# A fused adaLN attention block: the head's layernorm statistics, its order and its filler matmuls rearranged

## The chip, the cores and the metric

The kernel runs on one core of one Trainium2 chip. Its time is device microseconds of one execution, and the number that is compared is the median of several executions. A core has five engines that run their own instruction streams side by side: TensorE (PE; its weight loads are listed apart as PEld), VectorE (DVE), ScalarE (ACT), GpSimd (POOL) and SyncE (SP), which here only issues transfers. They meet at semaphores. 16 DMA engines move data between the main memory and the core's own memory (SBUF). TensorE writes into eight accumulation banks (PSUM), here `psbank0` to `psbank7`.

## What is computed

`x` is two batches of 256 tokens with 1152 channels, `c` one vector of 1152 for each batch; everything is bf16. The parts that matter:

```python
mod = (_silu(c) @ w_mod).reshape(B, 6, 1, D)
shift_a, scale_a, gate_a, shift_m, scale_m, gate_m = [mod[:, i] for i in range(6)]
h = _layernorm(x, axis=-1) * (1 + scale_a) + shift_a
qkv = h @ wqkv
...
p = _softmax(jnp.einsum('bqd,bkd->bqk', q, k) * D ** (-0.5), axis=-1)
a = jnp.einsum('bqk,bkd->bqd', p, v) @ wo
return x + gate_a * a
```

Only the first three of the six modulation vectors are used.

## The kernel before, in words

The 512 tokens are four tiles `i` of 128 rows (tiles 0 and 1 are batch 0, tiles 2 and 3 batch 1), and the 1152 channels are nine chunks `cc` of 128. Nothing is looped at run time: the program is written out instruction by instruction, in one Python function, and each engine runs its instructions in the order in which the function names them. A small helper (`_Prog`) records for every instruction what it reads and writes, and puts a wait wherever a value comes from another engine. For a PSUM bank it is stricter: whoever touches a bank waits for the last earlier access of every other engine to that bank. So the order around the change is the order of the calls in the source, and nothing else.

All loads are issued by SyncE in one list: four tiles of x, then, in four groups, the weights of the scale vector and the key weights of the same chunks ("ka"), then the shift weights, the remaining key weights, the query weights, the value weights. `c` is issued by ScalarE.

The head of the program, on which the change works, does this:

- `warm(n)` issues n matmuls of 512 columns on a tile of zeros into bank 4. Their result is not used. Before: five, then the nine tiny transposes of `c` (line 432), then nine more (all line 294).
- silu of `c`: a copy out of PSUM (`cT`), exp on ScalarE (`e1`), 1 + that on GpSimd (`d1`), a reciprocal on VectorE (`rc`) and a product on GpSimd (`scT`, line 457).
- Layernorm of tile i. `bn(i, q)` is VectorE's bn_stats over the third q of the channels (line 306). For tiles 1 to 3 the last third is taken by ScalarE instead: `third_act` gives the sum and the sum of squares (lines 312 and 314), and three tiny GpSimd steps, `third_end`, turn them into mean and sum of squared deviations (lines 318 to 322). Tile 0 takes all three thirds on VectorE. `aggr` merges the thirds (bn_aggr, line 330), `rstd` is a logarithm and an exp on ScalarE (lines 334 and 337), and `xn(i)` normalizes the tile on VectorE (line 341).
- `xT(i)` transposes the nine chunks of tile i on TensorE (line 349). Chunks 0 to 7 go to bank 5 for even tiles and bank 6 for odd ones, chunk 8 of every tile to bank 7. `xT_out(i, half, engine)` copies four chunks out of the bank (lines 300 on VectorE, 302 on ScalarE), and `xT_last(b, engine)` copies chunk 8 of both tiles of a batch. Tile 2 uses bank 5 again, so its transposes wait for both evacuations of tile 0; its ninth transpose goes to bank 7 and waits for `xT_last(0)`.
- `s_mm(g)` are the modulation matmuls for the scale vector, group g, two columns each (line 367), into bank 7; `s_ev` reads them and adds 1 (line 378); `scale_x` multiplies a transposed chunk of one batch with it (line 399 on VectorE, 401 on GpSimd, 403 on ScalarE).
- The key matmuls (line 419) follow: first chunks k = 0 and 1 of batch 0 (ten of 256 columns), then after the transposes of tiles 2 and 3 and `s_mm(1)` the same for batch 1 (ten of 256), then eleven of 512 columns, and so on through all chunks, with `s_mm` and the shift vector's `h_mm` between them.

The shift is added later (for queries and values); the queries, values, scores, softmax, the product with v, the output projection with the gate and the stores follow in one long run of matmuls.

Of the kernel before, what the change touches and what calls it, by code (L numbers as in the profile page):

```python
# [21 lines left out]
class _Prog:  # L22
# [12 lines left out]
    def op(self, eng, fn, r=(), w=(), dma=False, extra=()):  # L35
        o = _Op()
        o.eng, o.fn, o.dma = eng, fn, dma
        o.sem = o.val = None
        o.inc = False
        deps = set(extra)  # L40
        for k in r:
            if k[0] == "ps":
                continue
            p = self.last_w.get(k)
            if p is not None and not (p.eng == eng == PE):
                deps.add(p)
# [127 lines left out]
def _build(nc, es, x, c, wqkv, wo, w_mod, out):  # L174
# [33 lines left out]
    s1_sb = sb("s1_sb", [P, DC, 2], f32)  # L208
    sh_sb = sb("sh_sb", [P, DC, 2], f32)
    gaterow_sb = sb("gaterow_sb", [P, GW], bf16)  # L210
    stat_sb = sb("stat_sb", [P, TT, 6, 3], f32)
    sums_sb = sb("sums_sb", [P, TT, 2], f32)
    sq_sb = sb("sq_sb", [P, TT], f32)
    mv_sb = sb("mv_sb", [P, TT, 2], f32)
# [71 lines left out]
        out=ident[:, :], in_=ident[:, :], compare_op=ALU.not_equal, fill=1.0,  # L286
        base=0, pattern=[[-1, P]], channel_multiplier=1), r=[("ident",)], w=[("ident",)])
    op(POOL, lambda g: g.memset(eps_sb[:, :], EPS_B), w=[("eps",)])
    op(POOL, lambda g: g.memset(stat_sb[:, 1:TT, 4, 0:1], 384.0), w=[("cnt",)])
    op(POOL, lambda g: g.memset(scT_sb[:, :, :], 0.0), w=[("scT",)])  # L290

    def warm(n, bank=4):
        for _ in range(n):
            op(PE, lambda pe: pe.matmul(ps[bank][:, 0:512], warm_sb[:, 0:P], warm_sb[:, 0:512],  # L294
                                        start=True, stop=True),
               r=[("warm",)], w=[("ps", bank)])

    def evac(eng, dst, src, r, w):
        if eng == DVE:
            op(DVE, lambda v: v.tensor_copy(dst, src), r=r, w=w)  # L300
        else:
            op(AC, lambda a: a.activation(dst, src, ACT.Copy), r=r, w=w)  # L302


    def bn(i, q):
        op(DVE, lambda v: v.bn_stats(  # L306
            stat_sb[:, i, 2 * q:2 * q + 2, :].rearrange("p a b -> p (a b)"),
            x_sb[:, i, q * 384:(q + 1) * 384]), r=[("x", i)], w=[("stat", i, q)])

    def third_act(i):  # L310
        src = x_sb[:, i, 768:1152]
        op(AC, lambda a: a.activation(junk_sb[:, 0, :], src, ACT.Copy, accum_out=sums_sb[:, i, 0:1]),
           r=[("x", i)], w=[("junk", 0), ("sum", i)])
        op(AC, lambda a: a.activation(junk_sb[:, 1, :], src, ACT.Square, accum_out=sums_sb[:, i, 1:2]),  # L314
           r=[("x", i)], w=[("junk", 1), ("sq", i)])

    def third_end(i):
        op(POOL, lambda g: g.tensor_scalar(stat_sb[:, i, 4, 1:2], sums_sb[:, i, 0:1], 1.0 / 384, 0.0,
                                           op0=ALU.mult, op1=ALU.add), r=[("sum", i)], w=[("tm", i)])
        op(POOL, lambda g: g.tensor_tensor(sq_sb[:, i:i + 1], sums_sb[:, i, 0:1], sums_sb[:, i, 0:1],  # L320
                                           ALU.mult), r=[("sum", i)], w=[("s2", i)])
        op(POOL, lambda g: g.tensor_scalar(stat_sb[:, i, 4, 2:3], sq_sb[:, i:i + 1], -1.0 / 384,  # L322
                                           sums_sb[:, i, 1:2], op0=ALU.mult, op1=ALU.add),
           r=[("s2", i), ("sq", i)], w=[("tv", i)])

    def aggr(i, third):
        n = 5 if third else 6
        need = [("stat", i, 0), ("stat", i, 1)]
        need += [("tm", i), ("tv", i), ("cnt",)] if third else [("stat", i, 2)]
        op(DVE, lambda v: v.bn_aggr(mv_sb[:, i, :], stat_sb[:, i, 0:n, :].rearrange("p a b -> p (a b)")),  # L330
           r=need, w=[("mv", i)])

    def rstd(i):
        op(AC, lambda a: a.activation(lnv_sb[:, i:i + 1], mv_sb[:, i, 1:2], ACT.Ln,  # L334
                                      bias=eps_sb[:, 0:1], scale=1.0),
           r=[("mv", i), ("eps",)], w=[("lnv", i)])
        op(AC, lambda a: a.activation(rstd_sb[:, i:i + 1], lnv_sb[:, i:i + 1], ACT.Exp, scale=-0.5),
           r=[("lnv", i)], w=[("rstd", i)])

    def xn(i):  # L340
        op(DVE, lambda v: v.tensor_scalar(xo_sb[:, i, :], x_sb[:, i, :], mv_sb[:, i, 0:1],
                                          rstd_sb[:, i:i + 1], op0=ALU.subtract, op1=ALU.mult),
           r=[("x", i), ("mv", i), ("rstd", i)], w=[("xo", i)])

    def xT(i):
        for cc in range(DC):
            bank = (5 + i % 2) if cc < 8 else 7
            lo = cc * P if cc < 8 else 512 + i * P
            op(PE, lambda pe, cc=cc, bank=bank, lo=lo: pe.transpose(  # L349
                psb[bank][:, lo:lo + P], xo_sb[:, i, cc * P:(cc + 1) * P], ident[:, :]),  # L350
               r=[("xo", i), ("ident",)], w=[("ps", bank)])
# [20 lines left out]
    def s_mm(g):  # L372
        mod_mm(s_ap(g), [("ws", g)], *SGROUPS[g], 0)
# [18 lines left out]
    def scale_x(cc, b, eng):  # L392
        dst = h0T_sb[:, cc, b * NTOK:(b + 1) * NTOK]
        src = xnT_sb[:, cc, b * NTOK:(b + 1) * NTOK]
        sc = s1_sb[:, cc, b:b + 1]
        rk = [("xnT", cc, 2 * b), ("xnT", cc, 2 * b + 1), ("s1", cc)]
        wk = [("pv", cc, b)]
        if eng == DVE:
            op(DVE, lambda v: v.tensor_scalar(dst, src, sc, None, op0=ALU.mult), r=rk, w=wk)  # L399
# [24 lines left out]


    op(AC, lambda a: a.preload_act_table_set("natural_log_exp_and_others"))
    warm(5)

    def f_cT(pe):
        last = None  # L430
# [3 lines left out]
        return last  # L434
    op(PE, f_cT, r=[("c",), ("ident",)], w=[("ps", 0)])
    cT_ps = psb[0][:, 0:2 * DC].rearrange("p (k b) -> p k b", b=2)
    op(DVE, lambda v: v.tensor_copy(cT_sb[:, :, :], cT_ps), r=[("ps", 0)], w=[("cT",)])
    op(AC, lambda a: a.activation(e1_sb[:, :, :], cT_sb[:, :, :], ACT.Exp, scale=-1.0),
       r=[("cT",)], w=[("e1",)])
    warm(9)  # L440

    bn(0, 0)
    bn(0, 1)
    bn(0, 2)
    third_act(1)
    aggr(0, False)
    op(POOL, lambda g: g.tensor_scalar(d1_sb[:, :, :], e1_sb[:, :, :], 1.0, 1.0, op0=ALU.mult, op1=ALU.add),
       r=[("e1",)], w=[("d1",)])
    bn(1, 0)
    bn(1, 1)  # L450
    third_end(1)
    rstd(0)
    aggr(1, True)
    xn(0)
    rstd(1)
    op(DVE, lambda v: v.reciprocal(rc_sb[:, :, :], d1_sb[:, :, :]), r=[("d1",)], w=[("rc",)])
    op(POOL, lambda g: g.tensor_tensor(scT_sb[:, :, 0:2], cT_sb[:, :, :], rc_sb[:, :, :], ALU.mult),
       r=[("cT",), ("rc",)], w=[("scT",)])
    xn(1)
    third_act(2)  # L460
    bn(2, 0)
    bn(2, 1)
    third_end(2)
    xT(0)
    xT(1)
    s_mm(0)
    xT_out(0, 0, AC)
    xT_out(1, 0, DVE)
    s_ev(0)
    scale_x(0, 0, DVE)  # L470
    scale_x(1, 0, DVE)
    aggr(2, True)
    rstd(2)
    third_act(3)
    bn(3, 0)
    xn(2)
    bn(3, 1)
    third_end(3)
    aggr(3, True)
    rstd(3)  # L480
    xT_out(0, 1, AC)
    xn(3)
    xT_out(1, 1, DVE)
    xT_last(0, AC)

    for k in range(2):
# [248 lines left out]
```

## Time and profile before

| what | value |
|---|---|
| three runs, device time | 105.62, 104.95, 105.29 us |
| median | 105.29 us |
| the profiled execution, its own time | 105.28 us |
| its span, first to last instruction | 103.4 us |
| TensorE busy | 94.3 us (91%), 728 matmuls |
| VectorE, ScalarE, GpSimd busy | 44.8, 25.2, 8.7 us |
| mean granted TensorE clock over the span | 0.967 |
| DMA traffic | 21.65 MB, mean 209 GB/s |

The profile is one execution. Its times are microseconds from the first instruction, and line numbers are those of the kernel before. "Granted clock" is the share of full speed that TensorE's clock was given; where the records hold nothing earlier, the first stretch stands as full. A row of a timeline gives start, length, engine, line, operation, the tile written and those read, sizes, and the number of instructions merged; in square brackets stands how long the engine was idle before, and what ended that. A few matmul records can be missing. The chain of work that ended last is followed backward from the last instruction, at each step to whatever released it.

### The profile page before, as it was taken

How to read it: one execution, taken by the hardware profiler on the slowest of the kernel's cores; microseconds unless marked ns; L12 is line 12 of the kernel's file. 1: busy time of each engine (PE TensorE's matmuls, PEld its weight loads, DVE VectorE, ACT ScalarE, POOL GpSimd, SP SyncE). 2: the span in 40 equal slices, each digit the busy share in tenths (PEclk: the TensorE clock that was granted, in tenths of full speed). 3: DMA queues.
4: the chain of work that ended last, by engine and by line, in shares of the span. 5: the costliest groups of instructions: out<-in, count | busy, mean ns of one | idle time of the engine just before them, and what ended most of it. 6: DMA issues, size and time to landing. Idle time of an engine off the chain costs nothing.

```text
span 103.4 us, 1795 instructions
## 1 busy us (share of the span) xinstructions
PE 94.3 (91%) x728; PEld 55.8 (54%) x734; DVE 44.8 (43%) x122; ACT 25.2 (24%) x64; POOL 8.7 (8%) x30
## 2 busy tenths in 40 slices
PE   5956458999999999999999999999999999999990
PEld 2324356354545445454445688665667866666570
DVE  1598746012406905050372115660342755676572
ACT  4374584001105020000232135433103730000000
POOL 4022202001403004040000000000000000000000
PEclk9999985579999999999999999999999999999999
DMA  2999999999999999999999400002777666764122
GB/s 48 296 331 337 335 326 334 363 324 322 344 356 341 357 332 390 391 393 391 390 394 390 182 1 10 0 0 8 21 21 34 34 41 41 23 137 139 47 75 76
DMA packets 20076, 21.65 MB, mean 209 GB/s; under 512 B 866, under 2 KB 16098, under 8 KB 20068
## 3 DMA queue, kind: packets, MB, share of 16 engines
q1 hardware_dynamic: 20064, 21.53, 75.4%
q8 instruction: 6, 0.10, 0.4%
q10 hardware_dynamic: 4, 0.00, 0.1%
q14 instruction: 2, 0.02, 0.1%
HBM read 19.76 MB, written 1.18 MB: 203 GB/s over the span
## 4 chain that ended last, share of the span: by engine, by line
PE 83%; DMA 6%; DVE 3%; ACT 2%; SPq 2%; issue 1%; POOL 0%; POOLq 0%
PE psbank L419 35%; PE psbank L579 17%; PE psbank L685 17%; DMA wm_sb<-in_w_mod_dram 6%; PE psbank L592 4%; PE psbank L660 4%; PE psbank L367 4%; SPq L252 2%; PE psbank L637 1%; PE psbank L349 1%; DVE pvT_sb L399 1%; DVE ga_sb L692 1%; ACT lnv_sb L334 1%; DVE xo_sb L695 0%; ACT junk_sb L314 0%
## 5 line engine op out<-in xcount | busy, mean ns | idle before, releaser
L419 PE MATMUL psbank<-pvT_sb,wq_sb 128*128 128x512 bf16 (+1 forms) x88 | 20.6, 393 | 1.4 <-DVE pvT_sb L399 1.0
L579 PE MATMUL psbank<-wq_sb,hT_sb 128*128 128x384 bf16 x108 | 18.2, 326 | 0.1
L685 PE MATMUL psbank<-wm_sb,pvT_sb 128*128 128x384 bf16 (+2 forms) x117 | 17.7, 314 | 0.0
L419 PE MATMUL psbank<-hT_sb,wq_sb 128*128 128x512 bf16 x78 | 17.5, 379 | 0.1
L419 PEld LDWEIGHTS psbank<-pvT_sb,wq_sb 128*128 128x128 bf16 x91 | 9.5, 108 | 10.7 <-issue 2.4
L685 PEld LDWEIGHTS psbank<-wm_sb,pvT_sb 128*128 128x128 bf16 x117 | 11.2, 98 | 6.5
L579 PEld LDWEIGHTS psbank<-wq_sb,hT_sb 128*128 128x128 bf16 x108 | 10.5, 98 | 7.0 <-issue 0.2
L419 PEld LDWEIGHTS psbank<-hT_sb,wq_sb 128*128 128x128 bf16 x81 | 7.8, 98 | 9.1
L302 ACT ACTIVATE qkT_sb<-psbank 128x512 bf16<-128x512 f32 x8 | 4.3, 597 | 25.0 <-PE psbank L419 21.6
L692 DVE TENSOR_TENSOR ga_sb<-psbank,gate_rep 128x384 bf16<-128x384 f32 (+2 forms) x13 | 6.8, 527 | 6.1 <-PE psbank L685 6.1
L300 DVE CAST qkT_sb<-psbank 128x512 bf16<-128x512 f32 x10 | 6.3, 685 | 5.7 <-PE psbank L419 5.6
L300 DVE CAST v_sb<-psbank 128x384 bf16<-128x384 f32 x6 | 3.2, 555 | 10.9 <-PE psbank L579 10.9
L367 PEld LDWEIGHTS psbank<-scT_sb,wm_sb 128*128 128x128 bf16 x162 | 5.1, 97 | 1.6 <-POOL stat_sb L322 0.5
L294 PE MATMUL psbank<-warm_sb 128*128 128x512 bf16 x14 | 4.9, 506 | 1.2 <-DVE warm_sb L283 1.2
L349 PE MATMUL psbank<-ident,xo_sb 128*128 128x128 bf16 x36 | 2.6, 225 | 3.4 <-ACT xnT_sb L302 2.2
L367 PE MATMUL psbank<-scT_sb,wm_sb 128*128 128x2 bf16 x162 | 5.1, 164 | 0.3 <-DMA wm_sb<-in_w_mod_dram 0.3
L387 DVE COPY sh_sb<-psbank 128x6 f32<-128x6 f32 x3 | 0.5, 165 | 11.3 <-PE psbank L367 11.3
L302 ACT ACTIVATE v_sb<-psbank 128x384 bf16<-128x384 f32 x6 | 2.9, 487 | 9.8 <-PE psbank L579 9.8
L695 DVE TENSOR_TENSOR xo_sb<-x_sb,ga_sb 128x384 bf16<-128x384 bf16 (+2 forms) x13 | 4.5, 343 | 0.5
L306 DVE BATCH_NORM_STATS2 stat_sb<-x_sb 128x6 f32<-128x384 bf16 x9 | 4.5, 535 | 0.0
L378 DVE TENSOR_SCALAR s_sb<-psbank 128x4 f32<-128x4 f32 (+1 forms) x4 | 0.6, 160 | 8.8 <-PE psbank L367 8.8
L413 POOL TENSOR_SCALAR hT_sb<-pvT_sb,sh_sb 128x256 bf16<-128x256 bf16 x6 | 3.2, 533 | 14.8 <-DVE sh_sb L387 14.8
(57 smaller groups left out, 68.8 us busy)
## 6 DMA issues: line engine op xcount, KB each, us to landing
wm_sb<-in_w_mod_dram SPq DMA_DIRECT2D x4, 864.0 KB, 9.4
wq_sb<-in_wqkv_dram SPq DMA_DIRECT2D x4, 672.0 KB, 10.6
wq_sb<-in_wqkv_dram SPq DMA_DIRECT2D x3, 864.0 KB, 10.8
wm_sb<-in_w_mod_dram SPq DMA_DIRECT2D x1, 2592.0 KB, 15.9
wm_sb<-in_wo_dram SPq DMA_DIRECT2D x1, 2592.0 KB, 15.4
wm_sb<-in_w_mod_dram SPq DMA_DIRECT2D x3, 576.0 KB, 7.6
wq_sb<-in_wqkv_dram SPq DMA_DIRECT2D x3, 448.0 KB, 8.3
x_sb<-in_x_dram SPq DMA_DIRECT2D x4, 288.0 KB, 3.9
```

Of the source, the lines that this page charges most:

```text
L294: op(PE, lambda pe: pe.matmul(ps[bank][:, 0:512], warm_sb[:, 0:P], warm_sb[:, 0:512], start=True, stop=True), r=[("warm",)], w=[("ps", bank)])
L300: op(DVE, lambda v: v.tensor_copy(dst, src), r=r, w=w)
L302: op(AC, lambda a: a.activation(dst, src, ACT.Copy), r=r, w=w)
L306: op(DVE, lambda v: v.bn_stats(stat_sb[:, i, 2 * q:2 * q + 2, :].rearrange("p a b -> p (a b)"), x_sb[:, i, q * 384:(q + 1) * 384]), r=[("x ...
L367: op(PE, lambda pe, cc=cc, k=k: pe.matmul(ps[7][:, col + 2 * cc:col + 2 * cc + 2], src[:, k, (cc - a) * P:(cc - a + 1) * P], scT_sb[:, k, ...
L419: op(PE, lambda pe: pe.matmul(ps[bank][:, lo:hi], wq_sb[:, k, col * P:(col + 1) * P], src[:, k, lo:hi], start=(k == 0) if start is None el ...
L579: op(PE, lambda pe, k=k, q=q, bank=bank: pe.matmul(ps[bank][:, 0:384], hT_sb[:, k, i * P:(i + 1) * P], wq_sb[:, k, 2 * D + q * 384:2 * D + ...
L592: op(PE, lambda pe, cc=cc: pe.matmul(ps[bank][:, 0:NTOK], qkT_sb[:, cc, i * P:(i + 1) * P], qkT_sb[:, DC + cc, b * NTOK:(b + 1) * NTOK], s ...
L660: op(PE, lambda pe, h=h, cc=cc, sbk=sbk: pe.matmul(ps[bank][:, h * NTOK:(h + 1) * NTOK], v_sb[:, 2 * b + sbk, cc * P:(cc + 1) * P], pT_sb[ ...
L685: op(PE, lambda pe, i=i, k=k, c0=c0, c1=c1, n=n, bank=bank: pe.matmul(ps[bank][:, 0:n], pvT_sb[:, k, i * P:(i + 1) * P], wo_ap[:, k, c0:c1 ...
L692: op(DVE, lambda v, b=b, c0=c0, c1=c1, n=n, bank=bank, s=s: v.tensor_tensor(ga_sb[:, s, 0:n], ps[bank][:, 0:n], gate_rep[:, b, c0:c1], ALU ...
L695: op(DVE, lambda v, i=i, c0=c0, c1=c1, n=n, s=s: v.tensor_tensor(xo_sb[:, i, c0:c1], x_sb[:, i, c0:c1], ga_sb[:, s, 0:n], ALU.add), r=[("x ...
```

## The change

It does five things, all in the head.

1. Tile 0 is handled like the others: its last third goes to ScalarE and GpSimd, so `aggr` has one form and `stat_sb` five entries instead of six. `third_act` is called for one sum at a time.
2. `cT` is copied out of PSUM by ScalarE instead of VectorE, and `d1` follows at once.
3. The calls between c's transposes and the transposes of tile 2 are in another order: the statistics of tiles 2 and 3 come ahead of the evacuations and scales of batch 0, `rc` and `scT` come behind `xn(1)`, and `rstd(2)` stands before `xT_out(1, 0)`.
4. `xT_out(1, 1)` goes to ScalarE instead of VectorE; for batch 1, `xT_out(3, 1)` is called before `xT_out(2, 1)`.
5. The fillers become 4 + 13 + 2 + 3 instead of 5 + 9. The two stand ahead of `s_mm(0)`, the three behind it, ahead of batch 0's keys.

```diff
-    warm(5)
+    warm(4)
...
-    op(DVE, lambda v: v.tensor_copy(cT_sb[:, :, :], cT_ps), r=[("ps", 0)], w=[("cT",)])
+    evac(AC, cT_sb[:, :, :], cT_ps, [("ps", 0)], [("cT",)])
...
-    warm(9)
+    op(POOL, lambda g: g.tensor_scalar(d1_sb[:, :, :], e1_sb[:, :, :], 1.0, 1.0, op0=ALU.mult, op1=ALU.add),
+       r=[("e1",)], w=[("d1",)])
+    warm(13)
 
     bn(0, 0)
     bn(0, 1)
-    bn(0, 2)
-    third_act(1)
-    aggr(0, False)
...
+    third_act(0, 0)
+    third_act(0, 1)
+    third_end(0)
     bn(1, 0)
     bn(1, 1)
+    third_act(1, 0)
+    third_act(1, 1)
     third_end(1)
+    aggr(0)
     rstd(0)
-    aggr(1, True)
+    bn(2, 0)
+    third_act(2, 0)
+    aggr(1)
     xn(0)
     rstd(1)
+    xn(1)
...
-    xn(1)
-    third_act(2)
-    bn(2, 0)
+    third_act(2, 1)
+    third_end(2)
+    third_act(3, 0)
+    third_act(3, 1)
+    third_end(3)
     bn(2, 1)
-    third_end(2)
+    bn(3, 0)
+    aggr(2)
+    bn(3, 1)
     xT(0)
     xT(1)
+    warm(2)
     s_mm(0)
+    warm(3)
     xT_out(0, 0, AC)
+    rstd(2)
     xT_out(1, 0, DVE)
     s_ev(0)
     scale_x(0, 0, DVE)
     scale_x(1, 0, DVE)
-    aggr(2, True)
-    rstd(2)
-    third_act(3)
-    bn(3, 0)
     xn(2)
-    bn(3, 1)
-    third_end(3)
-    aggr(3, True)
+    aggr(3)
     rstd(3)
     xT_out(0, 1, AC)
     xn(3)
-    xT_out(1, 1, DVE)
+    xT_out(1, 1, AC)
     xT_last(0, AC)
...
+    xT_out(3, 1, DVE)
     xT_out(2, 1, AC)
-    xT_out(3, 1, DVE)
```

What this does to the engines' streams, in three places. Each row is a line of the source, the operation, what it writes and reads, its size, and how many follow each other. The lines of the kernel after are four lower in the helpers (330 is 326, 341 is 337, 378 is 374, 399 is 395, 334 is 330, 349 is 345, 367 is 363, 419 is 415).

VectorE, from the normalization of tile 0 or 1 to that of tile 3, before (`xo_sb` is the normalized tile, `mv_sb` its mean and variance, `stat_sb` the statistics of the thirds, `s_sb` the scale vector plus 1, `pvT_sb` the scaled chunk that the keys read):

```order
L456 RECIPROCAL rc_sb<-d_sb 128x18
L341 TENSOR_SCALAR xo_sb<-x_sb,mv_sb,rstd_sb 128x1152
L306 BN_STATS stat_sb<-x_sb 128x6 x2
L300 COPY xnT_sb<-psbank 128x4x128
L378 TENSOR_SCALAR s_sb<-psbank 128x4
L399 TENSOR_SCALAR pvT_sb<-xnT_sb,s_sb 128x256 x2
L330 BN_AGGR mv_sb<-stat_sb 128x2
L306 BN_STATS stat_sb<-x_sb 128x6
L341 TENSOR_SCALAR xo_sb<-x_sb,mv_sb,rstd_sb 128x1152
L306 BN_STATS stat_sb<-x_sb 128x6
L330 BN_AGGR mv_sb<-stat_sb 128x2
L341 TENSOR_SCALAR xo_sb<-x_sb,mv_sb,rstd_sb 128x1152
```

and VectorE at the same place after:

```order
L337 TENSOR_SCALAR xo_sb<-x_sb,mv_sb,rstd_sb 128x1152 x2
L458 RECIPROCAL rc_sb<-d_sb 128x18
L306 BN_STATS stat_sb<-x_sb 128x6 x2
L326 BN_AGGR mv_sb<-stat_sb 128x2
L306 BN_STATS stat_sb<-x_sb 128x6
L300 COPY xnT_sb<-psbank 128x4x128
L374 TENSOR_SCALAR s_sb<-psbank 128x4
L395 TENSOR_SCALAR pvT_sb<-xnT_sb,s_sb 128x256 x2
L337 TENSOR_SCALAR xo_sb<-x_sb,mv_sb,rstd_sb 128x1152
L326 BN_AGGR mv_sb<-stat_sb 128x2
L337 TENSOR_SCALAR xo_sb<-x_sb,mv_sb,rstd_sb 128x1152
```

The statistics of tiles 2 and 3 moved ahead of batch 0's evacuation, scale vector and scales; between batch 0's scales and the last normalization only tile 2's normalization and tile 3's aggregate are left.

ScalarE, from the evacuation of tile 0's first half to the end of batch 0's evacuations, before (`lnv_sb` and `rstd_sb` are the logarithm and the exp of a tile, `sums_sb` ScalarE's sums):

```order
L302 ACTIVATE xnT_sb<-psbank 128x4x128
L334 ACTIVATE lnv_sb<-mv_sb,eps_sb 128x1
L337 ACTIVATE rstd_sb<-lnv_sb 128x1
L312 ACTIVATE junk_sb,sums_sb<-x_sb 128x384
L314 ACTIVATE junk_sb,sums_sb<-x_sb 128x384
L334 ACTIVATE lnv_sb<-mv_sb,eps_sb 128x1
L337 ACTIVATE rstd_sb<-lnv_sb 128x1
L302 ACTIVATE xnT_sb<-psbank 128x4x128
L302 ACTIVATE xnT_sb<-psbank 128x256
```

and ScalarE at the same place after:

```order
L313 ACTIVATE junk_sb,sums_sb<-x_sb 128x384 x3
L302 ACTIVATE xnT_sb<-psbank 128x4x128
L330 ACTIVATE lnv_sb<-mv_sb,eps_sb 128x1
L333 ACTIVATE rstd_sb<-lnv_sb 128x1
L330 ACTIVATE lnv_sb<-mv_sb,eps_sb 128x1
L333 ACTIVATE rstd_sb<-lnv_sb 128x1
L302 ACTIVATE xnT_sb<-psbank 128x4x128 x2
L302 ACTIVATE xnT_sb<-psbank 128x256
```

Tile 3's sums moved ahead of the first evacuation, and two halves instead of one (tile 0's and tile 1's) stand between tile 3's rstd and the last chunk.

TensorE, from behind c's transposes to the transposes of tiles 2 and 3, after (before, the rows of 2 and 3 fillers are absent and the first row has 9):

```order
L294 MATMUL psbank<-warm_sb 128x512 x13
L345 MATMUL psbank<-ident,xo_sb 128x128 x18
L294 MATMUL psbank<-warm_sb 128x512 x2
L363 MATMUL psbank<-scT_sb,wm_sb 128x2 x18
L294 MATMUL psbank<-warm_sb 128x512 x3
L415 MATMUL psbank<-pvT_sb,wq_sb 128x256 x10
L345 MATMUL psbank<-ident,xo_sb 128x128 x18
```

Fillers now stand on both sides of the modulation matmuls; the order of all other matmuls is unchanged.

More of the change, by code (lines that the diff above doesn't have):

```diff
@@ L210, in _build @@
     gaterow_sb = sb("gaterow_sb", [P, GW], bf16)
-    stat_sb = sb("stat_sb", [P, TT, 6, 3], f32)
+    stat_sb = sb("stat_sb", [P, TT, 5, 3], f32)
     sums_sb = sb("sums_sb", [P, TT, 2], f32)
@@ L288, in _build @@
     op(POOL, lambda g: g.memset(eps_sb[:, :], EPS_B), w=[("eps",)])
-    op(POOL, lambda g: g.memset(stat_sb[:, 1:TT, 4, 0:1], 384.0), w=[("cnt",)])
+    op(POOL, lambda g: g.memset(stat_sb[:, :, 4, 0:1], 384.0), w=[("cnt",)])
     op(POOL, lambda g: g.memset(scT_sb[:, :, :], 0.0), w=[("scT",)])
@@ L308, in bn, with third_act @@
             x_sb[:, i, q * 384:(q + 1) * 384]), r=[("x", i)], w=[("stat", i, q)])
-    def third_act(i):
+    def third_act(i, kind):
         src = x_sb[:, i, 768:1152]
[L312 to L315, printed above, removed]
+        fn = (ACT.Copy, ACT.Square)[kind]
+        op(AC, lambda a: a.activation(junk_sb[:, kind, :], src, fn, accum_out=sums_sb[:, i, kind:kind + 1]),
+           r=[("x", i)], w=[("junk", kind), ("sum" if kind == 0 else "sq", i)])
     def third_end(i):
@@ L324, in third_end, with aggr @@
            r=[("s2", i), ("sq", i)], w=[("tv", i)])
[L326 to L331, printed above, removed]
+    def aggr(i):
+        op(DVE, lambda v: v.bn_aggr(mv_sb[:, i, :], stat_sb[:, i, :, :].rearrange("p a b -> p (a b)")),
+           r=[("stat", i, 0), ("stat", i, 1), ("tm", i), ("tv", i), ("cnt",)], w=[("mv", i)])
     def rstd(i):
@@ L436, in _build @@
     cT_ps = psb[0][:, 0:2 * DC].rearrange("p (k b) -> p k b", b=2)
-    op(DVE, lambda v: v.tensor_copy(cT_sb[:, :, :], cT_ps), r=[("ps", 0)], w=[("cT",)])
+    evac(AC, cT_sb[:, :, :], cT_ps, [("ps", 0)], [("cT",)])
     op(AC, lambda a: a.activation(e1_sb[:, :, :], cT_sb[:, :, :], ACT.Exp, scale=-1.0),
        r=[("cT",)], w=[("e1",)])
-    warm(9)
+    op(POOL, lambda g: g.tensor_scalar(d1_sb[:, :, :], e1_sb[:, :, :], 1.0, 1.0, op0=ALU.mult, op1=ALU.add),
+       r=[("e1",)], w=[("d1",)])
+    warm(13)
     bn(0, 0)
     bn(0, 1)
-    bn(0, 2)
-    third_act(1)
-    aggr(0, False)
-    op(POOL, lambda g: g.tensor_scalar(d1_sb[:, :, :], e1_sb[:, :, :], 1.0, 1.0, op0=ALU.mult, op1=ALU.add),
-       r=[("e1",)], w=[("d1",)])
+    third_act(0, 0)
+    third_act(0, 1)
+    third_end(0)
     bn(1, 0)
     bn(1, 1)
+    third_act(1, 0)
+    third_act(1, 1)
     third_end(1)
+    aggr(0)
     rstd(0)
-    aggr(1, True)
+    bn(2, 0)
+    third_act(2, 0)
+    aggr(1)
     xn(0)
     rstd(1)
+    xn(1)
     op(DVE, lambda v: v.reciprocal(rc_sb[:, :, :], d1_sb[:, :, :]), r=[("d1",)], w=[("rc",)])
```

## The prediction

> **What bounds the kernel now.** I read the slices of the page first, then the chain of work that ended last in order of time, then a table of TensorE's busy time by stretch, then the timelines of single engines.
>
> From the page: the busy tenths of TensorE and its granted clock, 40 slices of 2.585 us each.
>
> ```profile
> PE   5956458999999999999999999999999999999990
> PEclk9999985579999999999999999999999999999999
> ```
>
> From slice 7 on TensorE is full. Before that it has gaps, and in slices 6 to 9 its clock is far below full. So the end is set by when the dense stream starts and how fast it runs at first. The chain in order of time (start, length, what) names the place:
>
> ```profile
> 3.16 5.87 DMA wm_sb<-in_w_mod_dram
> ...
> 12.91 0.30 ACT lnv_sb L334
> ...
> 13.98 1.20 PE psbank L349 x17
> ...
> 15.21 0.44 DVE xnT_sb L300
> ...
> 15.67 0.30 DVE pvT_sb L399
> ...
> 16.01 2.31 PE psbank L419 x10
> ...
> 18.54 3.90 PE psbank L419 x10
> 22.44 0.43 PE psbank L367 x18
> ...
> 25.91 0.65 PE psbank L367 x27
> ...
> 26.64 4.48 PE psbank L419 x20
> ```
>
> Batch 1's chain runs through tile 3's rstd, the evacuation that frees a bank, the transposes of tiles 2 and 3 (13.98), an evacuation, a scale, and batch 1's first key matmuls (16.01). From there PE is never idle for long. The rows of 512-column keys differ: 20 matmuls of 512 columns take 4.48 us (0.224 each), while the 11 issued between 18.32 and 22.44 (the program's count; one record is missing) take 4.12. The next table gives per stretch: its length, then busy time and (instructions) of PE, PEld, DVE, ACT, POOL, the clock, the DMA share and GB/s. The edges are where the clock changes, and steps of 3.41 us from there.
>
> ```profile
> 1.29:4.70 3.41, 3.41 (x17) 1.18 (x17) 0.83 (x3) 1.61 (x3) 0.75 (x5) 1.00 0.81 223
> 4.70:8.12 3.42, 2.28 (x17) 1.02 (x15) 3.27 (x10) 2.66 (x11) 0.90 (x5) 1.00 1.02 322
> 8.12:11.53 3.41, 2.27 (x37) 1.94 (x37) 2.78 (x10) 1.70 (x7) 0.53 (x3) 1.00 1.10 331
> 11.53:14.95 3.42, 1.22 (x20) 0.98 (x18) 1.85 (x5) 2.22 (x9) 0.61 (x3) 0.99 1.13 329
> 14.95:18.36 3.41, 3.09 (x32) 2.33 (x31) 2.02 (x7) 1.66 (x4) 0.56 (x1) 0.50 1.08 340
> 18.36:21.77 3.41, 3.23 (x8) 1.21 (x8) 0.00 (x0) 0.00 (x0) 0.00 (x0) 0.51 1.08 356
> ```
>
> The stretch 11.53 to 14.95 is the emptiest on TensorE, and the clock is half for the 6.82 us behind it. The same table for the key matmuls alone (line 419; PE, PEld, clock, DMA):
>
> ```profile
> 8.12:11.53 3.41, 1.01 (x10) 0.90 (x10) 1.00 1.10 331
> 11.53:14.95 3.42, 0.24 (x3) 0.00 (x0) 0.99 1.13 329
> 14.95:18.36 3.41, 2.31 (x10) 1.64 (x12) 0.50 1.08 340
> ```
>
> A stretch with 1.01 us of keys held the clock, one with 0.24 lost it. TensorE's own timeline gives the rates:
>
> ```profile
> 1.19 2.31 PE L294 MATMUL psbank<-warm_sb 128*128 128x512 bf16 x5 [1.19 <-DVE warm_sb L283]
> ...
> 7.38 1.47 PE L349 MATMUL psbank<-ident,xo_sb 128*128 128x128 bf16 x18 [1.08 <-DVE xo_sb L341]
> ...
> 10.52 1.25 PE L419 MATMUL psbank<-pvT_sb,wq_sb 128*128 128x256 bf16 x10 [0.77 <-DVE pvT_sb L399]
> ...
> 15.07 0.67 PE L367 MATMUL psbank<-scT_sb,wm_sb 128*128 128x2 bf16 x18
> ```
>
> Ten keys of 256 columns take 1.25 us here and 2.31 at half clock. The first fillers take 0.46 each, half rate too, though the clock column says 1.00 there. Eighteen modulation matmuls take 0.67 at half clock.
>
> **The change, step by step.** Rows for VectorE, ScalarE and GpSimd:
>
> ```profile
> 3.95 1.47 DVE L306 BATCH_NORM_STATS2 stat_sb<-x_sb 128x6 f32<-128x384 bf16 x3
> 5.45 0.24 DVE L330 BATCH_NORM_AGGREGATE mv_sb<-stat_sb 128x2 f32<-128x18 f32 x1
> ...
> 7.24 0.26 DVE L456 RECIPROCAL rc_sb<-d_sb 128x18 f32<-128x18 f32 x1
> 7.49 0.63 DVE L341 TENSOR_SCALAR xo_sb<-x_sb,mv_sb,rstd_sb 128x1152 bf16<-128x1152 bf16 x1
> 8.04 1.00 DVE L306 BATCH_NORM_STATS2 stat_sb<-x_sb 128x6 f32<-128x384 bf16 x2
> 8.97 0.40 DVE L300 COPY xnT_sb<-psbank 128x512 bf16<-128x512 bf16 x1
> 9.79 0.16 DVE L378 TENSOR_SCALAR s_sb<-psbank 128x4 f32<-128x4 f32 x1 [0.41 <-PE psbank L367]
> 9.98 0.48 DVE L399 TENSOR_SCALAR pvT_sb<-xnT_sb,s_sb 128x256 bf16<-128x256 bf16 x2
> ```
> ```profile
> 4.59 0.52 ACT L312 ACTIVATE junk_sb<-x_sb 128x384 bf16<-128x384 bf16 x1 [0.30 <-DMA x_sb<-in_x_dram]
> ...
> 13.34 0.85 ACT L302 ACTIVATE xnT_sb<-psbank 128x512 bf16<-128x512 bf16 x2
> ```
> ```profile
> 12.35 0.27 POOL L322 TENSOR_SCALAR stat_sb<-sq_sb,sums_sb 128x1 f32<-128x1 f32 x1 [0.26 <-ACT junk_sb L314]
> ```
>
> *Tiles 0 and 1.* VectorE loses one bn_stats (0.49) and the copy of c ahead of the second normalization and gains tile 2's first bn_stats, so xn(1), at 7.49 now, starts at about 7.55; bounds 7.4 to 7.9, the upper if that bn_stats waits for tile 2's rows. ScalarE pays the copy of c and two more sums (0.52 each); GpSimd three more tiny steps (0.27 or less each). They lie beside VectorE's bn_stats and cost nothing; without that cover they would delay xn(0) by up to 1.
>
> *Tiles 2 and 3 on VectorE.* The reciprocal now follows xn(1), so the modulation matmuls are released at about 8.7 instead of 7.8; their weights, which land at 9.03 (the chain's DMA row), cover that. From 7.55: xn 0.55, reciprocal 0.25, two bn_stats 0.98, aggregate 0.15 (time to the next start), bn_stats 0.49, evacuation 0.40. The read of the modulation then starts at 10.37 instead of 9.79, the scales at 10.56, and batch 0's keys at 10.9 (a scale leads the keys by 0.34, 15.67 to 16.01), 0.38 later than now. They end at 12.15. What hides this is the bank that the next transposes wait for.
>
> *Batch 1's chain.* Read 0.19 and scales 0.43 put xn(2) at 10.99, the last aggregate at 11.49, ScalarE's logarithm at 11.77, and the evacuation of tile 0's second half 0.43 behind it (12.91 to 13.34 now), at 12.20. It ran at 13.34. The transposes follow 0.64 later, at 12.84. New: tile 1's second half is on ScalarE too, between this and the last piece, so ScalarE's three evacuations end at 12.20 + 0.85 + 0.50 = 13.55, and the ninth transpose of tile 2, in the bank of the last piece, waits for it, some 0.2 behind the eighth. Tile 3's nine (half of 1.47, say 0.7) end at 14.30, and 0.83 later (15.18 to 16.01 now) batch 1's keys start: 15.13, so **0.88 earlier**. Bounds: 0.1 (xn(1) at 7.9, and VectorE's steps at their whole lengths instead of the distance of their starts, 0.4 more) and 1.5 (no wait at the ninth, 0.6).
>
> *Fillers.* The 13 after c's transposes end near 7.0 (from 3.4, three at 0.46 and ten at 0.224), before tile 0's transposes, if the clock opens at 4.70 as now. The two ahead of the modulation (0.45) and the three ahead of the keys (0.67) fit before 9.35 and 10.6, when PE would wait: 0.2 at most on the modulation matmuls, covered by VectorE's queue. They matter by the clock alone. If it holds from 15.13 on, the ten keys cost 1.25 instead of 2.31 (**1.06 less**), the 11 behind them 11 x 0.224 = 2.46 instead of 4.12 (**1.66 less**).
>
> Sum: 0.88 + 1.06 + 1.66 = 3.60 off the profiled run's own 105.28 (span 103.4; median of the runs 105.29): **101.7 us**. The rest of the program moves up as a whole.
>
> Does the clock hold? In the changed kernel the stretch 11.53 to 14.95 would have some 0.6 us of keys, 0.6 of modulation matmuls and 1.4 of transposes. By PE's busy time (2.5) it is like the two that held (2.27, 2.28), by keys alone halfway between 0.24 and 1.01. I take holding, with no more than three in five.
>
> [...]
>
> **Rivals.**
> *The clock falls for one window all the same.* For: keys in that window are only 0.6; against: PE's busy time. At half from 14.95, keys from 15.2 to 17.5 (2.31), two of the 11 by 18.36 (0.448 each). The stretch from 14.95 to 18.36 is then full of keys, like the first row of the table, 3.41 full, behind which matmuls sped up; so nine more at 0.224 end at 20.4. Gain 2.0: **103.2**. [...]
>
> *The fillers don't help*, and half clock lasts to 21.77 as now: 17.5 plus 9.5 at 0.448, and 1.5 at 0.224, 22.1 against 22.44. Gain 0.3: **104.9**, no change.
>
> *The fillers run at half rate in front of the keys: slower.* Place: the stretch behind 8.12. Transposes 1.47 from 8.2 to 9.7, two fillers 0.92, modulation 0.67, three fillers 1.39, keys 2.31: 15.0; 18 transposes 2.94, modulation 0.67: 18.6; keys 2.31 to 20.9, two more by 21.77, nine at 0.224: 23.8 against 22.44. **106.6**. It decides if the clock is half at 8.12. Against: the stretch 4.70 to 8.12 held it with nine fillers, and now has four more.
>
> *Weights come too late.* Issues, and their time to landing, from SyncE's timeline and the line's own view, for the first key weights and those of k = 6:
>
> ```profile
> 3.63 0.68 SPq L263 DMA_DIRECT2D wq_sb<-in_wqkv_dram  x1
> ```
> ```profile
> DMA to landing us min/median/max: 6.8/6.8/6.8
> ```
> ```profile
> 11.79 2.60 SPq L263 DMA_DIRECT2D wq_sb<-in_wqkv_dram  x1
> ```
> ```profile
> DMA to landing us min/median/max: 10.6/10.6/10.6
> ```
>
> The first land at 10.43, so batch 0's keys can't gain anyway. The others land at 22.4; at full clock k = 6 comes at 15.13 + 1.25 + 2.46 + 0.43 + 14 x 0.224 + 0.65 + 7 x 0.224 = 24.6. It binds only from a gain of 5.8. If transfers slip by 3, it costs 0.8: 102.5.
>
> **How the numbers follow.** Clock holds (101.7) 0.57; one window lost (103.2) 0.28; weights late (102.5) 0.03; no help (104.9) 0.07; slower (106.6) 0.05. About 1% is what a measurement can tell from no change: faster 0.88, within 0.07, slower 0.05. Likeliest 101.7, its own range 100.9 (the ninth transpose doesn't wait, 0.6, and 0.2 for the run) to 102.5 (chain gains 0.1 only). The whole range reaches to 103.8, the lost window with 0.6 of a later chain, and leaves out less than 0.2.
>
> **What would show it.** A clock row without the dip of slices 6 to 9; batch 1's keys starting near 15.1, ten in 1.25; the modulation matmuls of 22.44 at 18.8; the ninth transpose of tile 2 waiting for ScalarE. Wrong would be: a half-clock stretch of 3.4 us or more behind 12, keys at 16 or later, or a DMA named as what the k = 6 keys waited for.

## The result and the profile after

| | before | after |
|---|---|---|
| median | 105.12 us (four executions, 104.65 to 105.62) | 101.44 us (four, 101.28 to 101.64) |
| profiled execution | 105.28 us, span 103.4 | 101.50 us, span 99.7 |
| mean granted clock of the span | 0.967 | 1.00 |

The ratio is 0.965, with a 95% interval of 0.960 to 0.970: 3.5% faster. The ratios with an interval leave out executions that stand over 1.5% above the fastest of their kernel; since some kernels below differ from execution to execution in just the clock that is studied here, their times are listed one by one, and the medians below are of all of them.

The slices of the page (here 2.49 us each), TensorE's busy tenths and its clock:

```profile
PE   5977979999999999999999999999999999999990
PEclk9999999999999999999999999999999999999999
```

The dip is gone. The chain in order of time (start, length, what), where before it ran from 12.91 to 22.44:

```profile
3.13 6.51 DMA wm_sb<-in_w_mod_dram
9.64 0.14 issue
9.77 0.60 PE psbank L363 x18
...
10.40 0.17 DVE s_sb L374
...
10.60 0.48 DVE pvT_sb L395 x2
11.08 0.49 DVE xo_sb L337
11.57 0.14 DVE mv_sb L326
...
11.73 0.30 ACT lnv_sb L330
...
12.26 1.26 ACT xnT_sb L302 x3
13.52 0.05 issue
13.57 0.69 PE psbank L345 x9
...
14.28 0.44 DVE xnT_sb L300
...
15.09 3.64 PE psbank L415 x21
18.73 0.43 PE psbank L363 x18
```

Three things are to be seen. Batch 1's keys start at 15.09 instead of 16.01. The 21 matmuls from there to the next modulation matmuls take 3.64 us instead of 6.43 (22.44 less 16.01). And the step ahead of the last transposes is ScalarE's third evacuation, which ends at 13.52. From 18.73 on nothing differs but the time: 22.44 less 18.73 is 3.71 us, and the spans differ by 3.7.

The table by stretch, again in steps of 3.41 us, from the one clock change that the records of this execution hold (4.37), and a row for the emptiest 3.41 us that can be found anywhere in the head. Columns: length, busy time and (instructions) of PE, PEld, DVE, ACT, POOL, then clock, DMA share, GB/s.

```profile
4.37:7.79 3.42, 2.89 (x19) 1.34 (x18) 2.82 (x8) 3.29 (x15) 1.22 (x6) 1.00 0.93 276
7.79:11.20 3.41, 2.73 (x39) 1.50 (x36) 3.01 (x11) 2.12 (x9) 1.37 (x7) 1.00 1.09 340
11.20:14.61 3.41, 2.77 (x46) 2.24 (x44) 1.41 (x4) 2.78 (x7) 0.00 (x0) 1.00 1.13 324
```
```profile
6.50:9.91 3.41, 2.23 (x28) 1.29 (x27) 3.02 (x10) 3.14 (x13) 1.37 (x7) 1.00 1.02 317
```

Before, the thinnest stretch had 1.22 us of TensorE work; in this execution the thinnest has 2.23, wherever it begins.

### The profile page after: what moved, and what is told of

Read it like the earlier page. It is cut to its first block, busy times and chain, and to the rows that moved or that the text cites. A ratio compares the mean times of both kernels' runs of the same rounds, so it can differ in the third digit from the quotient of the medians.

```text
span 99.7 us, 1825 instructions
## 1 busy us (share of the span) xinstructions
PE 93.7 (94%) x742; PEld 55.2 (55%) x742; DVE 43.7 (44%) x119; ACT 26.6 (27%) x70; POOL 9.3 (9%) x33
## 3 DMA queue, kind: packets, MB, share of 16 engines
HBM read 19.76 MB, written 1.18 MB: 210 GB/s over the span
## 4 chain that ended last, share of the span: by engine, by line
PE 83%; DMA 7%; DVE 3%; SPq 2%; ACT 2%; issue 1%
PE psbank L415 34%; PE psbank L582 18%; PE psbank L688 17%; DMA wm_sb<-in_w_mod_dram 7%; PE psbank L663 4%; PE psbank L595 4%; PE psbank L363 4%; SPq L252 2%; ACT xnT_sb L302 1%; PE psbank L640 1%; DVE pvT_sb L395 1%; PE psbank L345 1%; DVE ga_sb L695 1%; DVE xo_sb L698 1%; DVE xo_sb L337 0%
## 5 line engine op out<-in xcount | busy, mean ns | idle before, releaser
L415 PE MATMUL psbank<-pvT_sb,wq_sb 128*128 128x512 bf16 (+1 forms) x91 | 18.3, 355 | 0.4 <-DVE pvT_sb L395 0.4
L415 PE MATMUL psbank<-hT_sb,wq_sb 128*128 128x512 bf16 x81 | 18.0, 379 | 0.0
L415 PEld LDWEIGHTS psbank<-pvT_sb,wq_sb 128*128 128x128 bf16 x91 | 8.5, 97 | 8.6 <-DVE pvT_sb L395 0.9
L294 PE MATMUL psbank<-warm_sb 128*128 128x512 bf16 x22 | 6.8, 451 | 1.2 <-DVE warm_sb L283 1.2
L306 DVE BATCH_NORM_STATS2 stat_sb<-x_sb 128x6 f32<-128x384 bf16 x8 | 4.0, 537 | 3.0 <-DMA x_sb<-in_x_dram 3.0
L595 PE MATMUL psbank<-qkT_sb 128*128 128x256 bf16 x36 | 4.1, 272 | 0.0
L663 PE MATMUL psbank<-pT_sb,v_sb 128*128 128x256 bf16 x36 | 4.1, 273 | 0.0
```

Of the source, the lines that this page charges most:

```text
L306: op(DVE, lambda v: v.bn_stats(stat_sb[:, i, 2 * q:2 * q + 2, :].rearrange("p a b -> p (a b)"), x_sb[:, i, q * 384:(q + 1) * 384]), r=[("x ...
L415: op(PE, lambda pe: pe.matmul(ps[bank][:, lo:hi], wq_sb[:, k, col * P:(col + 1) * P], src[:, k, lo:hi], start=(k == 0) if start is None el ...
L595: op(PE, lambda pe, cc=cc: pe.matmul(ps[bank][:, 0:NTOK], qkT_sb[:, cc, i * P:(i + 1) * P], qkT_sb[:, DC + cc, b * NTOK:(b + 1) * NTOK], s ...
L663: op(PE, lambda pe, h=h, cc=cc, sbk=sbk: pe.matmul(ps[bank][:, h * NTOK:(h + 1) * NTOK], v_sb[:, 2 * b + sbk, cc * P:(cc + 1) * P], pT_sb[ ...
```

## The experiments

The theory: half of TensorE's clock was lost because a stretch of its program was too empty, and 2.7 of the 3.6 us come from not losing it; the rest is batch 1's earlier chain. Rivals: the earlier chain does it all; the new fillers do it all; only some kinds of work hold the clock.

Each row of the following table is one kernel; its executions stand with the mean clock of each. The half clock of the kernel before lasts 6.82 us (14.95 to 21.77), that of reorder_only 3.41 (11.89 to 15.30). Worked out from these lengths and the spans, one 3.41 us stretch at half clock makes 0.983, two make 0.967, three 0.95; 0.997 to 0.999 stand for some 0.6 us at half or less, in executions that are no longer than the others. The kernel before ran 29 times beside these, always at 0.948 to 0.967.

The mean clock is no witness by itself. The profiles of hole_mm, hole_tr, after_again and early_evac hold no clock record at all (their pages have no clock row), and their 1.000 stands for that; the key matmuls at the end of batch 1's chain, 3.64 to 3.85 us long in all four, show that they ran at full rate (3.64 in the profile after, with the clock at 1.00; 6.43 in the one before, with half up to 21.77). And one execution of no_2_3 has 0.983 at 101.65 us, no longer than its neighbour with 0.999; where its half stretch lay no trace shows.

```
kernel                 times, us (granted clock)
reorder_only           102.47 (0.983)  104.28 (0.967)  101.58 (0.997)  102.04 (0.980)
fillers_only           105.89 (0.967)  102.52 (1.000)  105.92 (0.967)  105.45 (0.967)
hole_mm                102.69 (1.000)  104.39 (0.983)  102.17 (1.000)  104.80 (0.983)
hole_tr                102.52 (1.000)  103.13 (1.000)  103.61 (0.983)  102.52 (1.000)
after_again            101.57  101.79  101.54  101.07  101.07  101.47 (0.999 to 1.000)
fillers_and_hole       103.00  102.66  102.85  102.69  102.80  102.40 (0.997 to 1.000)
early_evac             100.86  100.65  100.37  100.87  100.45  100.76 (0.997 to 1.000)
no_2_3                 103.55 (0.966)  101.64 (0.999)  103.78 (0.966)  101.65 (0.983)
fillers_and_hole_tr    102.91  103.05  103.08  102.65  103.30 (1.000)
nine_fillers           101.91  101.93  101.14  101.77  101.30  101.20 (0.997 to 1.000)
```

### The new order with the old fillers (reorder_only)

```diff
-    warm(4)
+    warm(5)
...
-    warm(13)
+    warm(9)
...
-    warm(2)
...
-    warm(3)
```

> The changed kernel with the old fillers (5 and 9, none around the modulation matmuls). If the earlier chain of batch 1 is enough to hold the clock, batch 1's keys start near 15.1 us, the clock stays 1.00 and the time is that of the changed kernel, 101.5 us. If the new fillers hold the clock (my theory), the 4.7 us without keys or fillers before batch 0's keys and the 3 us behind them let it fall for one window or two: 103.0 to 104.9 us, with batch 1's keys again near 15.1.

Its median is 102.26 us, 3.15 under the kernel before in the same comparison (105.41); the whole change brings 3.68. So the order alone brings most of the gain, more than the theory allowed (103.0 us at the least). The clock fell in three of four executions, for one stretch or for two. The table by stretch of its profile:

```profile
5.06:8.47 3.41, 2.25 (x19) 1.12 (x18) 2.76 (x9) 3.35 (x15) 1.04 (x6) 1.00 1.02 312
8.47:11.89 3.42, 1.57 (x32) 1.32 (x31) 2.83 (x9) 1.78 (x7) 1.36 (x7) 1.00 1.12 329
11.89:15.30 3.41, 3.41 (x31) 2.81 (x29) 0.85 (x4) 2.73 (x7) 0.00 (x0) 0.50 1.13 327
15.30:18.71 3.41, 3.06 (x36) 2.07 (x35) 1.99 (x7) 0.99 (x3) 0.56 (x1) 1.00 1.09 342
```

It fell, but at another place than in the kernel before: behind the thin stretch ahead of batch 0's keys (1.57 us of work). So the order alone closes the second thin stretch, and the first is then open. The half rate hits batch 0's keys (ten take 1.91 us, 1.25 in the kernel before) and the transposes (2.10, 1.49 in the changed kernel); with them that stretch is full (3.41), and behind it the clock was back at 1.00, after one stretch instead of two. The expectation of batch 1's keys near 15.1 missed: they start at 16.08, since the keys and transposes at half rate stand ahead of them.

### The old order with the new fillers (fillers_only)

```diff
-    warm(5)
+    warm(4)
...
-    warm(9)
+    warm(13)
...
     xT(1)
+    warm(2)
     s_mm(0)
+    warm(3)
```

> The kernel before, in its old order, with the new fillers (4, 13, 2 and 3). My theory: the old hole behind batch 0's keys (2.2 us idle, then 2 us of transposes and modulation matmuls) is untouched, so the clock falls as before and the time stays 105.1 us, within 0.5. Rival: fillers ahead of the keys are enough to hold the clock through the hole; then 2.7 us less, 102.4 us.

Median 105.67 us against 105.41 for the kernel before: no gain in three executions. The fourth kept its clock and took 102.52, as the rival had it; no trace of it shows why. The table by stretch of the profiled one:

```profile
8.66:12.08 3.42, 2.64 (x32) 1.58 (x31) 1.97 (x8) 0.88 (x4) 0.04 (x1) 1.00 1.12 330
12.08:15.49 3.41, 1.10 (x18) 0.91 (x17) 1.91 (x5) 2.20 (x9) 0.61 (x3) 1.00 1.13 329
15.49:18.90 3.41, 3.13 (x33) 2.44 (x32) 2.02 (x7) 1.73 (x4) 0.56 (x1) 0.50 1.09 343
```

Now the first thin stretch is closed (2.64) and the second is open (1.10), as in the kernel before. The two experiments mirror each other: each part closes one of two holes, and neither keeps the clock in every execution.

### The hole filled, with matmuls and with transposes (hole_mm, hole_tr, fillers_and_hole, fillers_and_hole_tr)

The old order; `EARLY` is 4 instead of 5, so that bank 4 is free for the filling (the same matmuls in another order). `hole_mm`:

```diff
-EARLY = 5
+EARLY = 4
...
             qk_mm("ka", h0T_sb, "pv", DC + j, k, j, b=0, start=(k == 0))
+    warm(10)
     xT(2)
```

> The kernel before, in its old order and with its old fillers, with ten filler matmuls in the hole between batch 0's keys and the transposes of tile 2 (bank 4 is kept free for them: 4 instead of 5 key columns are started early, the same work in another order). If the half clock comes from TensorE's emptiness there, the clock stays 1.00, batch 1's chain stays where it was (transposes near 14.0, keys near 16.0) and the time is 102.5 us. If the clock doesn't follow from it, 105.1 us.

`hole_tr` has 28 transposes of the identity tile in place of `warm(10)`:

```diff
+    def tr_fill(n):
+        for _ in range(n):
+            op(PE, lambda pe: pe.transpose(psb[4][:, 0:P], ident[:, :], ident[:, :]),
+               r=[("ident",)], w=[("ps", 4)])
...
+    tr_fill(28)
     xT(2)
```

> The same hole filled with 28 transposes of the identity tile (about as long) instead of ten filler matmuls. If any work on TensorE holds the clock, 102.5 us as with matmuls. If transposes don't count for it, as the emptiest stretch of the profile before suggests (0.97 us of transposes in it), the clock falls all the same: 105.1 us.

The medians are 103.54 us (`hole_mm`) and 102.83 (`hole_tr`). The executions that kept the clock took 102.2 to 103.1 us, and in the two profiles batch 1's keys start at 16.07 and 15.91, about where they were. TensorE's timeline of `hole_tr` (its lines are five higher than before; 424 are the keys):

```profile
11.30 1.73 PE L300 MATMUL psbank<-ident 128*128 128x128 bf16 x28
13.94 1.18 PE L354 MATMUL psbank<-ident,xo_sb 128*128 128x128 bf16 x18 [0.92 <-ACT xnT_sb L307]
15.91 3.85 PE L424 MATMUL psbank<-pvT_sb,wq_sb 128*128 128x256 bf16 x20 [0.36 <-DVE pvT_sb L404]
```

Keys at 15.91, their matmuls in 3.85, so the clock's share of the gain is there with the chain where it was. But the test was not clean: two executions of `hole_mm` and one of `hole_tr` still fell, for one stretch. Where, no trace shows; with the old fillers there are other thin stretches (in the profile of `hole_tr` 5.72 to 9.13 holds 1.77 us of TensorE work). So both were run again with the new fillers as well.

> The kernel before in its old order, with the new fillers (4, 13, 2, 3) and ten more in the hole behind batch 0's keys (4 instead of 5 key columns are started early). Both thin stretches are filled, so by busy time the clock is 1.00 in every execution and the time is 102.5 us, 1.0 over the changed kernel: that is what the earlier chain alone is worth. If the order itself matters for the clock, it falls in some executions (104 us or more).

> The old order with the new fillers and 28 transposes of the identity tile in the hole, in place of ten filler matmuls. All thin stretches but this one are filled, so it alone tells whether transposes hold the clock. If TensorE's busy time decides, whatever the work: clock 1.00 in every execution and 102.6 us, as with matmuls. If transposes don't count, the hole is as empty as before and the clock falls in most executions: 104 to 105.5 us.

With both holes closed the clock never fell: six of six with matmuls (median 102.75 us), five of five with transposes (103.05). Transposes held the clock in all five. The table by stretch of the profile with transposes, in steps of 3.41 us from the first change on record (6.31), shows it best: from 13.13 on there are transposes, modulation matmuls and the first 0.24 us of keys, and it held; 1.18 of the 2.13 us are the transposes of tiles 2 and 3, and without them less would be left than in any stretch that fell.

```profile
9.72:13.13 3.41, 3.36 (x53) 2.68 (x50) 2.37 (x8) 1.51 (x6) 0.61 (x3) 1.00 1.13 323
13.13:16.54 3.41, 2.13 (x45) 1.85 (x42) 2.02 (x7) 2.63 (x7) 0.00 (x0) 1.00 1.11 332
```

The full stretch 11.89 to 15.30 of `reorder_only` above says the same: 2.06 of its 3.41 us are transposes, and behind it the clock was back at 1.00.

Against the changed kernel in the same comparison (101.50), the kernel with matmuls in the hole is 102.75 - 101.50 = 1.25 us longer, 0.25 over the expectation. That is the chain's worth and two things beside it. The chain of its profile, of the longest of the six executions, shows them:

```profile
3.40 4.94 PE psbank L294 x13
8.34 1.00 PE psbank L349 x18
9.34 0.43 PE psbank L294 x2
9.78 0.44 PE psbank L367 x18
...
16.40 3.85 PE psbank L419 x21
```

The 13 fillers took 4.94 us in this execution (5.01 in TensorE's timeline, beside 3.47 in the changed kernel's; the first clock change on record is at 7.47, there at 4.37), so the transposes and the modulation matmuls came later, and in the old order VectorE takes up the chain of tiles 2 and 3 only behind those. Batch 1's keys start at 16.40, 0.39 later than in the kernel before. And the 21 key matmuls up to the next modulation take 3.85 us, 0.21 more than in the changed kernel, since with `EARLY` 4 two of batch 0's keys come later as parts of longer ones. This execution stands 1.52 us behind the changed kernel's profile at that point (20.25 for 18.73): 0.92 for the chain, 0.39 and 0.21 for the rest.

### What each filler is worth (no_2_3, nine_fillers)

```diff
-    warm(2)
     s_mm(0)
-    warm(3)
```

> The changed kernel without the two and the three fillers around the modulation matmuls; the 13 stay. The emptiest 3.41 us then hold about 2.0 us of TensorE work (18 transposes and 18 modulation matmuls), between what fell (1.57) and what held (2.25). If the bound lies above 2.0, some executions fall for one window and take 102 to 103.5 us; if below, all are at 101.4 us, and the five fillers are worth nothing.

The median is 102.60 us, the middle of two groups: two executions at 103.55 and 103.78 with two stretches lost, and two at 101.65, like the changed kernel. The table by stretch of the profile, one of the long ones, and TensorE's longest wait in it:

```profile
8.70:12.11 3.41, 1.84 (x28) 1.44 (x28) 2.55 (x10) 1.70 (x7) 0.83 (x4) 1.00 1.12 324
12.11:15.53 3.42, 2.77 (x38) 2.63 (x39) 1.42 (x5) 2.55 (x6) 0.00 (x0) 0.50 1.13 330
15.53:18.94 3.41, 3.41 (x14) 1.94 (x13) 1.04 (x4) 0.51 (x1) 0.56 (x1) 0.50 1.09 343
```
```profile
9.46 0.59 PE L363 MATMUL psbank<-scT_sb,wm_sb 128*128 128x2 bf16 x18 [0.87 <-POOL sq_sb L319]
```

A stretch with 1.84 us of work still lost the clock. The next, with 2.77, more than the 2.13 behind which it held elsewhere, didn't bring it back; behind the full one (3.41) it was back at 1.00. The longest single wait doesn't order these profiles: here none is over 0.87 us, while the kernel before held its clock through a stretch with a wait of 1.08 (the one ahead of 7.38), and the kernel with transposes through one of 0.92 (ahead of 14.33). So these five matmuls, whose result nobody reads, save 2 us in two of four executions and nothing in the other two, 1.1 on the medians.

```diff
-    warm(13)
+    warm(9)
```

> The changed kernel with nine fillers instead of 13 behind c's transposes; the two and the three stay. The emptiest 3.41 us then lie behind the ninth filler, with some 1.9 to 2.2 us of TensorE work, at the bound between what fell (1.84) and what held (2.23). If the bound is near 1.84, all executions are at 101.5 us and the four fillers are worth nothing here; if near 2.2, some fall for one window and take up to 103.8 us.

Median 101.54 us against 101.50 for the changed kernel, on another chip: the four extra fillers are worth nothing that could be measured. The emptiest stretch of its profile:

```profile
6.60:10.01 3.41, 1.78 (x20) 1.12 (x20) 3.02 (x10) 3.10 (x13) 1.37 (x7) 1.00 1.06 330
```

That is less than the 1.84 that fell, and yet six of six kept the clock. The profile doesn't contradict the other: the only change on record is at 5.32, and if the stretches are counted from there, neither of the next two is as empty.

```profile
5.32:8.73 3.41, 2.34 (x24) 1.37 (x23) 2.66 (x9) 3.25 (x14) 0.99 (x7) 1.00 0.94 282
8.73:12.14 3.41, 2.47 (x32) 1.35 (x30) 2.64 (x9) 1.25 (x5) 1.00 (x6) 1.00 1.12 339
```

Where they begin differs between executions (the first change on record lay at 4.37, 5.06, 5.32, 6.31 and 7.47 in five profiles). Whether an execution with a stretch that begins near 6.6 would fall, and make the four fillers worth something, stays open.

### The evacuations moved earlier (early_evac)

The chain after showed ScalarE's three evacuations behind tile 3's rstd. This kernel takes two of them forward, into time in which ScalarE idles (1.65 us ahead of 11.73 in the profile after), and gives the third to VectorE:

```diff
+    xT_out(0, 1, AC)
+    xT_last(0, AC)
     aggr(3)
     rstd(3)
-    xT_out(0, 1, AC)
+    xT_out(1, 1, DVE)
     xn(3)
-    xT_out(1, 1, AC)
-    xT_last(0, AC)
```

> The changed kernel with tile 0's second half and the last chunk evacuated by ScalarE ahead of tile 3's rstd, in time in which ScalarE idles, and tile 1's second half evacuated by VectorE between tile 3's aggregate and its normalization. If the bank's evacuation behind the rstd is what the transposes of tile 2 wait for, and the ninth waits for the last chunk, they now start when batch 0's keys end (near 12.3 instead of 12.8), batch 1's keys near 14.5 instead of 15.1, and the time is 100.9 us. If something else holds them (tile 3's normalization or the weights), 101.4 us.

Median 100.70 us (ratio 0.959, 0.953 to 0.965), beside 101.50 for the changed kernel (0.967, 0.961 to 0.972): faster than both kernels. Its longest execution (100.87) is under the shortest of the changed kernel in the same comparison (101.07). ScalarE's timeline and the chain:

```profile
9.81 0.58 ACT L302 ACTIVATE xnT_sb<-psbank 128x512 bf16<-128x512 bf16 x1
10.67 0.38 ACT L302 ACTIVATE xnT_sb<-psbank 128x256 bf16<-128x256 bf16 x1 [0.28 <-DVE s_sb L374]
```
```profile
12.37 0.59 DVE xo_sb L337
12.96 0.05 issue
13.01 0.63 PE psbank L345 x8
...
14.47 3.64 PE psbank L415 x21
```

The transposes no longer wait for a bank (they start at 12.19, with no wait behind batch 0's keys); those of tile 3 now wait 0.15 us for its normalization, and batch 1's keys start at 14.47, 0.62 earlier.

> The changed kernel itself, as measure for the others and to see whether its clock ever falls. Each stretch of 3.41 us in its profile has 2.23 us or more of TensorE work, wherever it begins. If busy time alone decides and the clock falls somewhere between 1.57 and 2.25 us of it, every execution keeps clock 1.00 and the times stay within 101.2 to 101.8 us. If keys and fillers alone count, one execution in three or so falls for one window and takes about 103 us.

The changed kernel itself, run six more times for this comparison, took 101.07 to 101.79 us, and by time and mean clock none of the six lost a stretch: with the four first, none of ten.

## Why the prediction was right, step by step

- **Batch 1's keys, 0.88 earlier.** Measured 0.92 (15.09 for 15.13). The chain went as told: ScalarE's evacuations end at 13.52 (13.55 forecast), and the ninth transpose of tile 2 waits for them. But that wait is smaller than the forecast's upper bound had it (0.6). The weight loads of the ninth and of tile 3's transposes show it:

```profile
13.56 0.56 PEld L345 LDWEIGHTS psbank<-ident,xo_sb 128*128 128x128 bf16 x10 [0.31 <-ACT xnT_sb L302]
```

Without it the chain would gain some 0.3. The kernel with the evacuations moved starts batch 1's keys 0.62 earlier, but it takes away two waits, this one and the 0.50 us ahead of tile 2's first transpose, and then waits for tile 3's normalization instead; no run takes away the ninth's wait alone.
- **The clock, 1.06 + 1.66.** Measured 6.43 - 3.64 = 2.79 against 2.72, 2.7% of the 105.28. The experiments that fill the hole in the old order show that it is the clock and not the chain.
- **Batch 0's keys, 0.38 later and hidden.** They start at 11.06, 0.54 later. One input was off: the first modulation weights land at 9.64 in this execution, not at 9.03, so those matmuls start at 9.77 and the three fillers end only when the keys begin. TensorE's timeline, up to 14.0:

```profile
10.22 0.81 PE L294 MATMUL psbank<-warm_sb 128*128 128x512 bf16 x3
11.06 1.25 PE L415 MATMUL psbank<-pvT_sb,wq_sb 128*128 128x256 bf16 x10
12.80 1.38 PE L345 MATMUL psbank<-ident,xo_sb 128*128 128x128 bf16 x16 [0.50 <-ACT xnT_sb L302]
```

The 0.50 us in which the transposes wait for ScalarE's evacuation hide it. VectorE reads the modulation at 10.40 (10.37 forecast), and that this came out so near is partly luck. The forecast had VectorE's own queue decide; its evacuation, at 9.86 for 0.40, ends at 10.26, and what decides are the late modulation matmuls, which end at 10.37. So the late weights cost some 0.1 here, but the chain after begins with that transfer, and a later one costs: in the profile with nine fillers those matmuls start at 10.21, 0.44 later, and batch 1's keys at 15.52, 0.43 later.
- **Tiles 0 and 1 at no cost.** xn(1) started at 7.45 (7.55 forecast).
- **The doubt about the clock.** That the clock held was a bet in the forecast, at three in five, because keys alone in the stretch 11.53 to 14.95 lay halfway. That was the wrong measure: transposes and fillers counted too (2.13 us, most of it transposes, held the clock in the profile of fillers_and_hole_tr), and by all work no stretch in the changed kernel's profile is under 2.23 us. The forecast's own row from 4.70 says as much: it has no key, only fillers and transposes (2.28 us), and the clock held. The rival of one lost window never occurred in ten executions, so its price of 103.2 is not tested; the changed kernel without the five fillers took 103.55 and 103.78, but with two stretches lost.
- **The rival that fillers don't help** was half right in a way the forecast didn't see. Fillers alone help the old order in one execution of four, and the order alone mostly loses the clock at the other hole. Of the fillers, the five near the modulation matmuls matter, the four added to the nine don't show.
- **Slower by fillers at half rate** needed a half clock behind 8.12. The row from 7.79 has 1.00.
- **Weights too late** was right to be small: in the profile after the keys' matmuls and weight loads waited for scaled chunks alone (three waits, 1.3 us together), never for a transfer.

## What to carry to other kernels

Look at the granted clock beside the chain, in stretches as long as the records show them (3.41 us here): a wait of 2.2 us on TensorE cost another 2.8 us here, in matmuls behind it at half rate. Close every thin stretch, not only the one where the profile shows the fall; with the order alone or the fillers alone, each closing one of the two holes, the clock still fell in three of four executions. Before spending fillers, look for evacuations that stand behind an unrelated wait on an idle engine: moving three calls was worth 0.80 us, beside the 0.92 by which the rearranged statistics brought batch 1's keys forward.

## What the runs showed of the hardware

In stretches of 3.41 us, counted from a clock change on record, TensorE's busy time tells the ones that lost the clock from those that held it in these profiles, whichever of the work here it is (fillers, transposes, modulation matmuls, keys): it fell behind 1.10 (fillers_only), 1.22 (before), 1.57 (reorder_only) and 1.84 us (no_2_3), and held behind 2.13 (fillers_and_hole_tr), 2.25 (reorder_only), 2.27 and 2.28 (before). (The rows of the kernel before begin 0.05 us late, as 0.99 and 0.51 in their clock column show; 0.05 earlier they read 1.21, 2.22 and 2.33.) The number of instructions doesn't order them: 32 in one that fell (1.57), 17 in one that held (2.28). The 1.84 is 54% of its stretch, so one that was more than half busy lost the clock all the same. The clock came back behind full stretches (3.41 us; 3.20 and 3.23 at half rate in two profiles where a matmul's record is missing); 2.77, 3.09 and 3.13 us, with waits of 0.28 to 0.54 us in them, didn't bring it back. The changed kernel's first change on record (4.37) follows 3.18 us of work, with TensorE not yet started for the first 0.23 us, so not quite every stretch that brought it back was full. And in the records the clock column says 1.00 from the start of the span, while the first fillers take 0.46 to 0.47 us each (five in 2.31 before, four in 1.89 after), twice the 0.224 of a matmul of 512 columns at 1.00: what stands ahead of the first recorded change is not a measurement.
